# Chunked attention feeding a snake MLP: a V load moved to a later pass, a reordered front, half-tile sines and a split last store

## The chip, the core and the metric

The kernel runs on one core of one Trainium2 chip. The metric is the device time of one execution in microseconds (us). The kernel before took 225.47 us as the median of 8 runs (222.81 to 227.42).

## The reference

Two layers are computed one after the other. The first is attention over chunks of 32 positions: each chunk sees its own 32 keys, 16 to the left, 8 to the right and 8 memory keys. The second is an MLP whose activation is the snake function. B = 4, H = 8, S = 768, D = 64; the MLP has 3072 tokens (4 batches of 768), 512 inputs and 2048 hidden channels.

```
for c in range(nc):                       # chunk 32, left 16, right 8
    k_full = concat([mem_k, k[l_start:r_end]]);  v_full = concat([mem_v, v[l_start:r_end]])
    a = exp(scale * q_c @ k_full.T - max);  a = a / sum(a)
    out[c] = a @ v_full
x = out.transpose(0, 2, 1, 3).reshape(B * S, H * D)
h = x @ w_in
g = h + sin(alpha * h) ** 2 / alpha
y = g @ w_out
```

## The kernel before, in words

The work goes batch by batch. For each batch, the attention makes `xT` (the attention's output, transposed, 128 channels x 4 x 768 tokens); then a pass ("layer", L660) of 16 tiles of 128 hidden channels makes `gT`; then `second` (L545) multiplies `gT` by `w_out` in six tiles of 128 tokens, and each finished 128x512 tile is copied from PSUM to `o_sb` and stored by a DMA from SP's queue. The order of all instructions is written out by hand: a program order per engine, with matmuls of the previous batch's second product fed in small portions (`Feed`, L20) between the steps of the next batch's attention and pass, so that TensorE (PE) always has something to do.

A tile of the pass is: 8 matmuls of 128x384 (`half_first`, L506, four for each half of the tokens) into a pair of PSUM banks; one sine by ScalarE (ACT, L528); one square by ACT (L532), VectorE (DVE, L535) or GpSimd (POOL, L535), chosen by the letters A, V, P of a string; and one DVE operation that forms u*u/alpha + h into `gT` (L538, "the snake" below). PSUM has eight banks; in the first two passes four pairs go around, so tile n + 4 cannot begin before the snake of tile n has read its banks.

**The front (batch 0).** q and k are transposed on PE, scores are taken by unit (head pair, half of the tokens), their exponentials by ACT (L356), products with V on PE (L368), a reciprocal and a multiplication on DVE (L374, L375), a transposition on PE (L385) and a copy into `xT` by ACT (L388). ACT's exponential and sine lie in different tables; L460 loads the sine's between two of the copies. At the end `ahead` (L517) issues the first halves of tiles 0, 1 and 2 on PE; the rest of these tiles follows in the pass.

**Batches 1 to 3.** `attention` (L473) takes scores of eight blocks j of 96 queries (L283), exponentials on ACT (L296), products with V (L309) and the division on DVE. The first five blocks reach `xT` by a transposing DMA from SP, the others by PE and DVE. At its end `ahead` issues the first halves of three tiles. For batches 2 and 3, k and q rows are loaded by 22 DMAs from POOL's queue (`load_rows`, L138) into `kst` and `qst` and turned by 14 transposing DMAs from SP's queue (`cross_steps`, L161, lines 164 and 167) during the pass of the batch before. V is loaded by POOL's DMAs (`load_v`, L177; line 183, and 200 for a tail of batch 3). In the kernel before, the pass of batch 1 starts (L718) by loading the rows of batch 2 and behind them, on the same queue, V of batch 3; the pass of batch 2 loads the rows of batch 3 (L724). `gate` is a one-element copy on POOL that holds these loads back until the attention has written `xT`.

## Time and profile before

| | us |
|---|---|
| median of 8 runs (lowest, highest) | 225.47 (222.81, 227.42) |
| the profiled execution's own time | 225.95 |
| its span, first to last instruction | 224.2 |
| PE / ACT / DVE / POOL busy | 211.2 / 148.0 / 136.0 / 82.5 |
| last matmul of the program | ends about 219.3 |

The execution runs in stages, by the time at which their first matmul starts: the front to 25.7, the pass of batch 0 to 48.2, the attention of batch 1 with the end of batch 0's second product to 74.2, the pass of batch 1 to 97.8, the attention of batch 2 from 99.2 to 115.8, the pass of batch 2 with the second product of batch 1, the attention of batch 3 from 149.2, its pass to 197.4, and the last second product. In rows of the timeline the columns are start, duration, engine, line, operation, tiles, shapes and count, then in brackets the idle time of that engine ahead of the row and what ended it. In windows a row gives the stretch and its length, then busy time (and count) of each engine, the granted TensorE clock, the DMA share and GB/s.

### The profile page before, as it was taken

To read this page: it belongs to the slowest core of one execution; us is meant where nothing else is said; L and a number is where in the kernel's file an instruction comes from. 1 tells how busy PE (TensorE), PEld (TensorE's weight loads), DVE (VectorE), ACT (ScalarE), POOL (GpSimd) and SP (SyncE) were. 2 spreads that over 40 slices of the span, in tenths; PEclk is the share of its full clock that TensorE was granted. 3 is DMA by queue.
4 is the path that set the end of the run, shared out by engine and by line. 5 is a ranking of instruction groups with operands and counts; after the bars stand their busy time and mean duration, and the time that the engine had idled before them with its cause. 6 is when DMAs were issued, how large, how long until landed. Compare 5 with 4: busy or idle time off the path is not lost.

```text
span 224.2 us, 4377 instructions
## 1 busy us (share of the span) xinstructions
PE 211.2 (94%) x1672; PEld 112.7 (50%) x1672; DVE 136.0 (61%) x233; ACT 148.0 (66%) x217; POOL 82.5 (37%) x102
## 2 busy tenths in 40 slices
PE   7999799999999989999599999999999999999991
PEld 2555555545545545544255555544555555544440
DVE  5866559793437689995562875765845764851110
ACT  2558578994778399998546879797928777741101
POOL 8997663795600799800039960000000000000000
PEclk9999999999999999999999999999999999999999
DMA  5999999999999799999969999552410110112121
GB/s 80 166 163 175 207 207 207 200 174 123 101 175 166 68 174 145 159 153 123 171 111 141 130 104 208 132 134 71 115 52 0 47 50 1 47 47 80 64 94 48
DMA packets 98733, 26.96 MB, mean 120 GB/s; under 512 B 86792, under 2 KB 95640, under 8 KB 98712
## 3 DMA queue, kind: packets, MB, share of 16 engines
q0 software_dynamic: 71520, 14.82, 81.2%
q1 hardware_dynamic: 27192, 11.86, 26.8%
q8 instruction: 13, 0.21, 0.4%
q14 instruction: 8, 0.07, 0.1%
HBM read 29.69 MB, written 6.29 MB: 161 GB/s over the span
## 4 chain that ended last, share of the span: by engine, by line
PE 64%; DMA 10%; POOL 7%; SPq 6%; DVE 5%; ACT 4%; issue 2%; DVEq 0%; ACTq 0%; POOLq 0%
PE ps L554 33%; PE ps L508 23%; DMA kT<-kst 5%; DMA q_bf<-in_q_dram 3%; SPq L167 3%; SPq L164 3%; PE ps L283 2%; PE ps L309 2%; DMA kst<-in_k_dram 2%; DVE gT L538 1%; POOL kst L148 1%; ACT u L528 1%; POOL qst L153 1%; POOL kst L143 1%; POOL vw L183 1%
## 5 line engine op out<-in xcount | busy, mean ns | idle before, releaser
L554 PE MATMUL ps<-w_out_sb,gT 128*128 128x512 bf16 x384 | 98.9, 379 | 0.3
L508 PE MATMUL ps<-xT,w_in_sb 128*128 128x384 bf16 x512 | 91.3, 326 | 1.9 <-DVE gT L538 1.3
L538 DVE SCALAR_TENSOR_TENSOR gT<-u,inv_alpha,ps 128x768 bf16<-128x768 f32 x64 | 63.4, 1012 | 24.1 <-ACT u L532 20.0
L528 ACT ACTIVATE u<-ps,alpha_sb 128x768 f32<-128x768 f32 x64 | 56.7, 896 | 26.7 <-PE ps L508 25.8
L508 PEld LDWEIGHTS <-w_in_sb 128*128 128x128 bf16 x512 | 49.6, 98 | 39.7 <-issue 4.2
L554 PEld LDWEIGHTS <-gT 128*128 128x128 bf16 x384 | 34.4, 98 | 31.3 <-issue 0.9
L532 ACT ACTIVATE u<-u 128x768 f32<-128x768 f32 x40 | 33.7, 843 | 1.2
L296 ACT ACTIVATE pt<-ps,biasm 128x256 bf16<-128x256 f32 x72 | 28.7, 473 | 7.2 <-issue 2.8
L567 DVE COPY o_sb<-ps 128x512 f32<-128x512 f32 x17 | 11.7, 690 | 25.3 <-PE ps L554 25.2
L535 DVE TENSOR_TENSOR u<-u 128x768 f32<-128x768 f32 x18 | 17.2, 954 | 6.0 <-ACT u L528 5.9
L183 POOL DMA_DIRECT2D vw<-in_v_dram x15 | 18.1, 1215 | 0.0
L316 DVE TENSOR_TENSOR x_blk<-ps,rinv 96x512 bf16<-96x512 f32 x24 | 16.5, 686 | 1.1 <-DVE rinv L315 0.3
L569 ACT COPY o_sb<-ps 128x512 f32<-128x512 f32 x7 | 4.1, 584 | 19.0 <-PE ps L554 19.0
L336 PE MATMUL ps<-idle 128*128 128x512 bf16 x31 | 10.9, 454 | 1.7 <-DVE vw L596 1.2
L262 ACT COPY kT<-ps 128x672 bf16<-128x672 bf16 x8 | 5.7, 718 | 10.0 <-PE ps L247 7.1
L148 POOL DMA_DIRECT2D kst<-in_k_dram x16 | 11.8, 735 | 0.1
L283 PEld LDWEIGHTS <-kT 64*128 64x128 bf16 x192 | 4.9, 94 | 13.0 <-issue 11.2
L143 POOL DMA_DIRECT2D kst<-in_k_dram x16 | 11.3, 704 | 0.3 <-issue 0.3
L315 DVE RECIPROCAL rinv<-ps 96x8 f32<-96x8 f32 x24 | 4.8, 202 | 10.6 <-PE ps L309 5.4
L309 PEld LDWEIGHTS <-pt 128*128 128x128 bf16 x192 | 9.0, 98 | 4.1
L153 POOL DMA_DIRECT2D qst<-in_q_dram x12 | 10.9, 908 | 0.0
L535 POOL TENSOR_TENSOR u<-u 128x768 f32<-128x768 f32 x6 | 8.9, 1492 | 5.3 <-ACT u L528 5.3
(77 smaller groups left out, 132.8 us busy)
## 6 DMA issues: line engine op xcount, KB each, us to landing
out_dram<-o_sb SPq DMA_DIRECT2D x24, 256.0 KB
w_out_sb<-in_moe_w_out_dram POOLq DMA_DIRECT2D x2, 1024.0 KB, 17.6
w_in_sb<-in_moe_w_in_dram POOLq DMA_DIRECT2D x3, 512.0 KB, 10.1
vw<-in_v_dram POOLq DMA_DIRECT2D x3, 512.0 KB, 10.6
qst<-in_q_dram POOLq DMA_DIRECT2D x12, 128.0 KB, 4.8
vw<-in_v_dram POOLq DMA_DIRECT2D x2, 448.0 KB, 12.4
kst<-in_k_dram POOLq DMA_DIRECT2D x14, 64.0 KB, 5.0
kst<-in_k_dram POOLq DMA_DIRECT2D x14, 56.0 KB, 4.8
```

Of the source, the lines that this page charges most:

```text
L143: nc.gpsimd.dma_start(kst[r0:64, j, :].rearrange("p (h d) -> p h d", d=D), k[b, :, lo + r0:lo + 64, :].rearrange("h p d -> p h d"),)
L148: nc.gpsimd.dma_start(kst[72:72 + n, j, :].rearrange("p (h d) -> p h d", d=D), k[b, :, QW * j + 48:QW * j + 48 + n, :].rearrange("h p d -> ...
L183: nc.gpsimd.dma_start(vw[p0:p1, c0:c1, 0:D], flat[r0:r0 + QW * (c1 - c0)].rearrange("(n t) d -> t n d", t=QW)[0:p1 - p0],)
L296: nc.scalar.activation(pt[:, 0:H * QW].rearrange("p (g e c) -> p g e c", g=2, e=4)[:, :, :, 32 * m:32 * m + 32], sc[:, :, 0:4 * QW].rearra ...
L309: nc.tensor.matmul(otv[:, e, hp, :], pt[:, QW * i:QW * i + P], vws[b % 2][:, 2 * hp + e, j, 0:D + 1],)
L316: nc.vector.tensor_tensor(out=x_blk[:].rearrange("p g e d -> p e g d"), in0=otv[0:QW, :, :, 0:D], in1=rinv[:].unsqueeze(3).to_broadcast([Q ...
L508: nc.tensor.matmul(hT[:, hf, 0:HALF], w_in_sb[:, kt, P * ft:P * ft + P], xT[:, kt, HALF * hf:HALF * hf + HALF], start=(kt == 0), stop=(kt ...
L528: nc.scalar.activation(u[:], hT[:, :, 0:HALF], ACTF.Sin, scale=alpha_sb[:, ft:ft + 1])
L532: nc.scalar.activation(u[:], u[:], ACTF.Square)
L535: eng.tensor_tensor(out=u[:], in0=u[:], in1=u[:], op=ALU.mult)
L538: nc.vector.scalar_tensor_tensor(out=gT[:, ft, :].rearrange("p (e c) -> p e c", e=2), in0=u[:], scalar=inv_alpha[:, ft:ft + 1], in1=hT[:, ...
L554: nc.tensor.matmul(ps[:, bank, :], gT[:, ft, P * s:P * s + P], w_out_sb[:, ft, :], start=(ft == 0), stop=(ft == FT - 1),)
```

## The change

There are four edits.

1. `load_v(3)`, three DMAs of POOL's queue, goes from the pass of batch 1 (behind the rows of batch 2) to the pass of batch 2 (behind its gate, ahead of the rows of batch 3).
2. The last output tile (128 tokens x 512) is made in two halves of 256 columns, each with 16 matmuls, a copy (DVE the first, ACT the second) and a store of its own.
3. `ahead` does more: to the first half of a tile's matmuls it adds, on ACT, the sine and the square of that half; the snakes of these halves stand on DVE at the start of the pass, and `first` then handles only the second half of these tiles. Batches 1 to 3 do so for three tiles, batch 0 for two.
4. In the front, products with V, scores, copies and idle matmuls (`warm`) stand in another order; the sine's table is loaded behind the last ACT copy; the last copy into `xT` goes from ACT to DVE. In the pass of batch 0 the string of squares, the tile at which the ring of PSUM pairs is widened, and the tile at which V of batch 1 is issued (12 instead of 11) change.

```diff
@@ -379,15 +379,13 @@
         )
         return x_blk
 
-    def unit_turn(xT, hp, half, x_blk):
+    def unit_turn(xT, hp, half, x_blk, copy):
         xtp = packed(single(), 4, QW)
         for jj in range(4):
             nc.tensor.transpose(
                 xtp[:, jj, :], x_blk[:, jj].rearrange("p e d -> p (e d)"), ident[0:QW, 0:QW]
             )
-        nc.scalar.copy(
-            xT[:, hp, HALF * half:HALF * half + HALF].rearrange("p (j c) -> p j c", j=4), xtp
-        )
+        copy(xT[:, hp, HALF * half:HALF * half + HALF].rearrange("p (j c) -> p j c", j=4), xtp)
 
     def attention_first(kq, alphas, ahead):
         xT = xp.tile([P, KT, S], BF, name="xT")
@@ -411,8 +409,8 @@
         def pv(*u):
             xb[u] = unit_values(*u, pt[u])
 
-        def x(*u):
-            unit_turn(xT, *u, xb.pop(u))
+        def x(hp, half, copy=nc.scalar.copy):
+            unit_turn(xT, hp, half, xb.pop((hp, half)), copy)
 
         turn_k(0)
         warm(2)
@@ -450,24 +448,26 @@
         warm(1)
         plan(big=(4, 0, 2))
         pv(1, 0)
-        sc(3)
-        units = [(hp, half) for hp in range(1, HP - 1) for half in range(2)]
-        for n in range(1, len(units)):
-            pv(*units[n])
-            warm(1)
-            x(*units[n - 1])
-            if n == 1:
-                nc.scalar.preload_act_table(ACTF.Sin)
-            warm(1)
+        sc_half(3, 0)
+        pv(1, 1)
+        sc_half(3, 1)
+        x(1, 0)
+        pv(2, 0)
         warm(1)
+        x(1, 1)
+        pv(2, 1)
+        warm(2)
+        x(2, 0)
         pv(3, 0)
+        warm(2)
         x(2, 1)
         pv(3, 1)
+        warm(1)
         x(3, 0)
+        nc.scalar.preload_act_table(ACTF.Sin)
         ahead(0, 0, xT)
+        x(3, 1, nc.vector.tensor_copy)
         ahead(1, 0, xT)
-        x(3, 1)
-        ahead(2, 0, xT)
         return xT
 
     def attention(b, stream, shares, lag, crossed, beside=iter(()), beside_from=0):
@@ -514,33 +514,45 @@
 
     begun = {}
 
+    def sine(u, hT, ft, e):
+        nc.scalar.activation(u[:, e], hT[:, e, 0:HALF], ACTF.Sin, scale=alpha_sb[:, ft:ft + 1])
+
     def ahead(ft, hf, xT):
         if ft < 3:
-            begun[ft] = two("big")
-            half_first(begun[ft], ft, hf, xT)
-
-    def first(ft, xT, gT, square, hT=None):
-        if hT is None:
+            hT = two("big")
+            half_first(hT, ft, hf, xT)
+            u = mlp.tile([P, 2, HALF], F32, name="u", bufs=4)
+            e = slice(hf, hf + 1)
+            sine(u, hT, ft, e)
+            nc.scalar.activation(u[:, e], u[:, e], ACTF.Square)
+            begun[ft] = (hT, u)
+
+    def first(ft, xT, square, started=None):
+        e = slice(0, 2)
+        if started is not None:
+            hT, u = started
+            e = slice(1, 2)
+        else:
             hT = two("h")
             half_first(hT, ft, 0, xT)
+            u = mlp.tile([P, 2, HALF], F32, name="u", bufs=4)
         half_first(hT, ft, 1, xT)
-        u = mlp.tile([P, 2, HALF], F32, name="u", bufs=4)
-        nc.scalar.activation(u[:], hT[:, :, 0:HALF], ACTF.Sin, scale=alpha_sb[:, ft:ft + 1])
+        sine(u, hT, ft, e)
 
         def squared():
             if square == "A":
-                nc.scalar.activation(u[:], u[:], ACTF.Square)
+                nc.scalar.activation(u[:, e], u[:, e], ACTF.Square)
             else:
                 eng = nc.vector if square == "V" else nc.gpsimd
-                eng.tensor_tensor(out=u[:], in0=u[:], in1=u[:], op=ALU.mult)
-
-        def finish():
-            nc.vector.scalar_tensor_tensor(
-                out=gT[:, ft, :].rearrange("p (e c) -> p e c", e=2),
-                in0=u[:], scalar=inv_alpha[:, ft:ft + 1], in1=hT[:, :, 0:HALF],
-                op0=ALU.mult, op1=ALU.add,
-            )
-        return squared, finish
+                eng.tensor_tensor(out=u[:, e], in0=u[:, e], in1=u[:, e], op=ALU.mult)
+        return hT, u, e, squared
+
+    def snake(gT, ft, hT, u, e):
+        nc.vector.scalar_tensor_tensor(
+            out=gT[:, ft, :].rearrange("p (e c) -> p e c", e=2)[:, e],
+            in0=u[:, e], scalar=inv_alpha[:, ft:ft + 1], in1=hT[:, e, 0:HALF],
+            op0=ALU.mult, op1=ALU.add,
+        )
 
     def second(i, gT, cut=0):
 
@@ -569,12 +581,32 @@
                 nc.scalar.copy(o_sb[:], ps[:, bank, :])
             nc.sync.dma_start(out[S * i + P * s:S * i + P * s + P, :], o_sb[:])
 
+        def halves(s):
+            for hf in range(2):
+                bank = begin_o()
+                c = slice(256 * hf, 256 * hf + 256)
+                for ft in range(FT):
+                    nc.tensor.matmul(
+                        ps[:, bank, 0:256], gT[:, ft, P * s:P * s + P], w_out_sb[:, ft, c],
+                        start=(ft == 0), stop=(ft == FT - 1),
+                    )
+                    if ft % 2 == 1 and (hf == 0 or ft < FT - 1):
+                        yield
+                kept.remove(bank)
+                o_sb = mlp.tile([P, d_model], F32, name="o_sb", bufs=2)
+                (nc.vector.tensor_copy if hf == 0 else nc.scalar.copy)(o_sb[:, 0:256], ps[:, bank, 0:256])
+                nc.sync.dma_start(out[S * i + P * s:S * i + P * s + P, c], o_sb[:, 0:256])
+
         early = []
         if cut:
             for s in range(2):
                 early.append(begin_o())
                 yield from part(s, early[s], 0, cut)
         for s in range(NSUB):
+            if i == B - 1 and s == NSUB - 1:
+                yield from halves(s)
+                yield
+                break
             bank = early[s] if s < len(early) else begin_o()
             yield from part(s, bank, cut if s < len(early) else 0, FT)
             end_o(s, bank)
@@ -661,35 +693,37 @@
         gT = gTs[i % 2]
         pend = []
         fed = 0
+        for ft in sorted(begun):
+            snake(gT, ft, *begun[ft], slice(0, 1))
         for ft in range(FT):
             begin(ft)
             square = squares[ft % len(squares)]
-            squared, fin = first(ft, xT, gT, square, begun.pop(ft, None))
+            hT, u, e, squared = first(ft, xT, square, begun.pop(ft, None))
             want = to_feed * (ft + 1) // FT
             feed.take(want - fed)
             fed = want
             for due, f in [p for p in pend if p[0] <= ft]:
-                f()
+                snake(gT, *f)
             pend = [p for p in pend if p[0] > ft]
             squared()
-            pend.append((ft + (2 if square == "P" else 1), fin))
+            pend.append((ft + (2 if square == "P" else 1), (ft, hT, u, e)))
         for due, f in pend:
-            f()
+            snake(gT, *f)
         feed.add(second(i, gT, 0 if i else 13), NSUB * FT)
 
     prs = []
 
     def begin_0(ft):
-        if ft == 3:
-            plan(h=[6] + rings["big"])
-        if ft == 11:
+        if ft == 2:
+            plan(h=[rings["big"][0], 6] + rings["big"][1:])
+        if ft == 12:
             load_v(1)
             send_memv(1)
             send_memv(2)
         if ft == 15:
             prs.extend(pair_up(kq1[n // HP], n % HP) for n in range(4))
 
-    layer(0, xT, "VPPAPAVPPAPAVAAA", begin_0, 0)
+    layer(0, xT, "VPPAPAVPAVPPAAAA", begin_0, 0)
     last4 = rings["h"]
     plan(one=(last4[0], last4[0] + 1), t=(last4[1], last4[1] + 1), big=last4[1:])
     put_memk(1)
@@ -718,12 +752,12 @@
             if i == 1 and ft == 0:
                 nc.gpsimd.tensor_copy(gate[:], xT[0:1, 0, QW * 6 - 1:QW * 6])
                 load_rows(2)
-                load_v(3)
                 for _ in crossings:
                     pass
             if i == 2:
                 if ft == 0:
                     nc.gpsimd.tensor_copy(gate[:], xT[0:1, 0, QW * 6 - 1:QW * 6])
+                    load_v(3)
                     load_rows(3)
                 if ft >= 1:
                     next(crossings, None)
```

On POOL, this is the piece between the rows of batch 2 and those of batch 3 (`gate` is the one-element copy, `vw_88` the buffer of V for odd batches, `kst` the rows of k; in the kernel before the lines are 183, 200 and 726):

```order
 L143 DMA kst<-in_k_dram 64x8x64
 L148 DMA kst<-in_k_dram 48x8x64
+L759 COPY gate<-xT 1x1
 L183 DMA vw_88<-in_v_dram 64x64x64
 L183 DMA vw_88<-in_v_dram 56x63x64
 L200 DMA vw_88<-in_v_dram 48x64
-L726 COPY gate<-xT 1x1
 L143 DMA kst<-in_k_dram 48x8x64
 L148 DMA kst<-in_k_dram 56x8x64
```

The three V loads now stand behind the gate of batch 2's pass and ahead of the first rows of batch 3.

On ACT, from the last exponentials of the front to the first tiles of the pass, first as before (388 is the copy into `xT`, 460 the table load, 528 the sine, 532 the square):

```order
L356 ACTIVATE pt_first<-ps 128x768 x2
L388 COPY xT<-ps 128x384
L460 ACT_TABLE_LOAD
L388 COPY xT<-ps 128x384 x5
L528 ACTIVATE u<-ps,alpha_sb 128x768 x4
L532 ACTIVATE u<-u 128x768
```

and in the changed kernel (467 is the table load, 518 the sine, 527 the square inside `ahead`):

```order
L356 ACTIVATE pt_first<-ps 128x768 x2
L388 COPY xT<-ps 128x384 x5
L467 ACT_TABLE_LOAD
L518 ACTIVATE u<-ps,alpha_sb 128x384
L527 ACTIVATE u<-u 128x384
L518 ACTIVATE u<-ps,alpha_sb 128x384
L527 ACTIVATE u<-u 128x384
L518 ACTIVATE u<-ps,alpha_sb 128x384 x2
L518 ACTIVATE u<-ps,alpha_sb 128x768 x2
```

The table load stands behind five copies, not between the first and the others, and the first sines and squares are of 384 columns.

On DVE, from the last copy into `xT` of batch 1 into its pass, before (535 is the square, 538 the snake):

```order
L329 COPY xT<-ps 128x4x96
L535 TENSOR_TENSOR u<-u 128x768
L538 SCALAR_TENSOR_TENSOR gT<-u,inv_alpha,ps 128x768 x2
L535 TENSOR_TENSOR u<-u 128x768
L538 SCALAR_TENSOR_TENSOR gT<-u,inv_alpha,ps 128x768 x2
```

and in the changed kernel (547 the square, 551 the snake):

```order
L329 COPY xT<-ps 128x4x96
L551 SCALAR_TENSOR_TENSOR gT<-u,inv_alpha,ps 128x384 x3
L547 TENSOR_TENSOR u<-u 128x384
L551 SCALAR_TENSOR_TENSOR gT<-u,inv_alpha,ps 128x384 x2
L547 TENSOR_TENSOR u<-u 128x384
L551 SCALAR_TENSOR_TENSOR gT<-u,inv_alpha,ps 128x384
L551 SCALAR_TENSOR_TENSOR gT<-u,inv_alpha,ps 128x768
L547 TENSOR_TENSOR u<-u 128x768
```

Three half snakes stand ahead of the first square; nothing on DVE waits for a whole tile until they are through.

## The prediction

> **What bounds the kernel now.** I read the windows first, to see where TensorE (PE) is not busy, then PE's timeline for the waits inside those windows, then the chain of waits and the DMA view.
>
> ```profile
> 20.00:32.00 12.00, 10.34 (x113) 6.33 (x112) 6.56 (x13) 8.36 (x13) 7.38 (x9) 1.00 1.30 204
> ...
> 78.00:98.00 20.00, 18.98 (x114) 10.86 (x112) 18.24 (x20) 19.07 (x24) 16.70 (x21) 1.00 1.97 157
> 99.00:112.00 13.00, 10.52 (x127) 4.99 (x125) 8.19 (x15) 10.17 (x23) 0.00 (x0) 1.00 1.74 148
> 113.00:149.00 36.00, 36.00 (x228) 19.85 (x223) 22.70 (x30) 27.32 (x34) 16.71 (x23) 1.00 1.27 135
> ...
> 219.00:224.00 5.00, 0.19 (x1) 0.00 (x0) 0.00 (x0) 0.59 (x1) 0.00 (x0) 0.95 0.14 54
> ```
>
> The second number is the length, the third PE's busy time. From 113 us on PE is gapless: nothing that the change does there can gain, it can only cost. What can be had lies in four places: the front (1.66 us idle of 12), the pass of batch 1 (1.02 of 20, with DVE and ACT almost full as well), the attention of batch 2 (2.48 of 13), and the 4.9 us behind the last matmul. Each of the four edits aims at one of them.
>
> **Edit 1: V of batch 3 leaves the pass of batch 1.** PE's rows of scores, for batch 2 (first, second, seventh, eighth block) and for batch 3 (first, last):
>
> ```profile
> 99.16 0.34 PE L283 MATMUL ps<-qT,kT 64*128 64x96 bf16 x8
> 100.68 0.34 PE L283 MATMUL ps<-qT,kT 64*128 64x96 bf16 x8 [0.21 <-DVE gT L538]
> ...
> 109.62 0.35 PE L283 MATMUL ps<-qT,kT 64*128 64x96 bf16 x8 [1.23 <-DVE o_sb L567]
> ...
> 112.25 0.34 PE L283 MATMUL ps<-qT,kT 64*128 64x96 bf16 x8 [1.28 <-DMA kT<-kst]
> ...
> 149.19 0.34 PE L283 MATMUL ps<-qT,kT 64*128 64x96 bf16 x8
> ...
> 159.35 0.34 PE L283 MATMUL ps<-qT,kT 64*128 64x96 bf16 x8
> ```
>
> First to last block takes 13.09 us for batch 2 and 10.16 for batch 3, with the same matmuls between. Of the 2.93 us, 0.21 are a wait for a snake; 2.7 are two waits for turned rows of k and q (the copy named in the first is done long before; the transposition of the sixth q tile is what is late there too). Why are they late?
>
> ```profile
> 100.49 1.29 SPq L167
> ...
> 101.90 10.30 DMA kT<-kst
> ...
> vw<-in_v_dram POOLq DMA_DIRECT2D x2, 448.0 KB, 12.4
> ...
> vw<-in_v_dram POOLq DMA_DIRECT2D x1, 441.0 KB, 21.0
> ...
> 90.79 3.36 POOL L183 DMA_DIRECT2D vw<-in_v_dram  x2
> 94.13 0.56 POOL L200 DMA_DIRECT2D vw<-in_v_dram  x1
> ...
> 70.43 2.51 SPq L492 DMA_TRANSPOSE xT<-x_blk  x2
> ...
> 74.19 0.81 PE L508 MATMUL ps<-xT,w_in_sb 128*128 128x384 bf16 x4 [0.18 <-DMA xT<-x_blk]
> ```
>
> The last transposition is issued at 101.90 and lands 10.30 us later, while V of batch 3 (issued 90.8 to 94.7, 21 us to landing for its second part) fills the same DMA engines. With those engines nearly free, the second of the two transpositions issued from 70.43 on (about 71.7) lets PE go at 74.19: 2.5 us. So without V the last one lands near 104.4. It is needed at 99.16 + 10.16 = 109.3, or 108.1 if the pass ahead gets 1.25 us shorter (below): a cover of 3.7 us. I take the whole **2.7 us**. Ends: 2.9 (the 0.21 too), 0 (the rows of batch 2, not V, hold the transpositions up).
>
> Its new place, in batch 2's pass:
>
> ```profile
> 115.55 0.18 POOL L726 COPY gate<-xT 1x1 bf16<-1x1 bf16 x1 [20.85 <-DVE xT L329]
> ...
> 132.03 0.64 POOL L148 DMA_DIRECT2D kst<-in_k_dram  x1
> ...
> kst<-in_k_dram POOLq DMA_DIRECT2D x14, 56.0 KB, 4.8
> ...
> 148.35 1.21 SPq L164 DMA_TRANSPOSE kT<-kst  x1
> ...
> POOL w_in_sb L220 <- DMA q_bf<-in_q_dram: 0.9, 1, 0.9
> ```
>
> Three V issues put the rows back by 3.36 + 0.56 = 3.9 us at POOL. More comes from completion semaphores: the program has eight for POOL's DMAs, so each issue waits for the landing of the one eight before it (the last row is such a wait). The sixth row DMA then waits for V's first part: 12.4 us by the median of V alone. The 22 row DMAs took 17.1 us behind the gate (to 132.67), 0.78 each; now the sixth is issued 12.4 us behind the gate, the seventh with V's second part at 14.1, fifteen more at 0.78: the last at 25.8, landing 4.8 later, at 30.6 (146.2 on the old clock). SP turns them in order and issued the last at 148.35, that is after this moment; landing 2.5 us later, 8.5 us ahead of its need at 159.35. V itself is first used after the scores of 149.19 and is there by about 130. Behind the transpositions on SP stand stores of batch 1's output, with two `o_sb` buffers: they leave when they left before. So I cost the new place at **0**; what hides it is that 8.5 us, and beyond it each us is one us of PE.
>
> **Edits 3 and 4 in the front.** Tile 4 of batch 0's pass waits for the snake of tile 0:
>
> ```profile
> 21.85 1.28 ACT L460 ACT_TABLE_LOAD   x1
> 23.15 0.86 ACT L388 COPY xT<-ps 128x384 bf16<-128x384 bf16 x2
> ...
> 21.89 0.20 DVE L374 RECIPROCAL rinv<-ps 96x8 f32<-96x8 f32 x1
> ...
> 25.63 0.69 DVE L375 TENSOR_TENSOR x_blk<-ps,rinv 96x512 bf16<-96x512 f32 x1
> ...
> 27.63 0.48 ACT L388 COPY xT<-ps 128x384 bf16<-128x384 bf16 x1 [1.23 <-PE ps L385]
> 28.94 3.50 ACT L528 ACTIVATE u<-ps,alpha_sb 128x768 f32<-128x768 f32 x4 [0.82 <-PE ps L508]
> ...
> 30.94 1.01 DVE L538 SCALAR_TENSOR_TENSOR gT<-u,inv_alpha,ps 128x768 bf16<-128x768 f32 x1
> ...
> 32.01 16.07 PE L508 MATMUL ps<-xT,w_in_sb 128*128 128x384 bf16 x96 [0.51 <-DVE gT L538]
> ...
> 48.23 4.48 PE L554 MATMUL ps<-w_out_sb,gT 128*128 128x512 bf16 x20
> ```
>
> Before: last division ends 26.32, last copy 28.1, first sine 28.94, snake 31.95. After, step by step: a unit costs DVE about 0.93 (0.20, a short gap, 0.69); with V products ahead of scores and no table load between copies, I place the last division's end at 25.3. PE turns it (0.15), DVE copies (0.35): xT is whole at 26.1 and the second halves start at 26.2, not 28.1. ACT copies until 25.2 and loads its table until 26.5; two half sines and half squares at 0.5 take it to 28.5; the second half's sine ends at 29.0, square 29.65, snake 30.25. Tile 4 starts at 30.3: **1.7 us** earlier. The same 12 tiles follow (16.2 us to 48.23), so the pass ends that much earlier. Half operations go by these rows:
>
> ```profile
> L388 ACT COPY xT<-ps 128x384 bf16<-128x384 bf16 x8 | 3.7, 480 | 2.7 <-PE ps L385 2.7
> L329 DVE COPY xT<-ps 128x384 bf16<-128x384 bf16 x9 | 3.2, 352 | 1.8 <-PE ps L326 1.8
> ```
>
> Ends: 1.9 (the 1.66 us that PE idles there and a warm-up matmul), 0.3 (the new order saves only a warm-up matmul).
>
> A page speaks against this: the Trainium skill (ScalarE: Activation LUTs, "What ACT_TABLE_LOAD costs") gives a table switch 1283 ns plus a drain of about 1380. The load above took 1.28 us and the next copy began 0.02 us behind it, so this trace shows no drain; by the page the front's term would be 0.3.
>
> **Edit 3 in the passes.** Pass of batch 1:
>
> ```profile
> 77.94 0.90 ACT L528 ACTIVATE u<-ps,alpha_sb 128x768 f32<-128x768 f32 x1 [3.85 <-PE ps L508]
> 78.87 0.96 DVE L535 TENSOR_TENSOR u<-u 128x768 f32<-128x768 f32 x1 [1.83 <-ACT u L528]
> 81.00 2.76 PE L508 MATMUL ps<-xT,w_in_sb 128*128 128x384 bf16 x16 [0.50 <-DVE gT L538]
> ```
>
> ACT idles 3.85 us and DVE 1.83 just before a stretch in which both are the bound. The change moves into these idle times three half sines and three half squares (ACT) and three half snakes (DVE). From 78 on ACT then has, per tile of the three, about 0.9 - 0.5 less sine, and half a square less for one: 3 x 0.4 = 1.2, and about 0.4, less some 0.35 of start costs that halves pay twice: **1.25 us**. DVE is rid of more (three half snakes and two half squares, 2.5 us), so ACT limits. Ends: 0.4 (start costs eat it), 2.2 (DVE's share counts). In the passes of batches 2 and 3 the halves cost ACT about 0.1 us a tile; it is busy 27.32 of 36 us there, which hides it: 0.
>
> **Edit 2, the tail.**
>
> ```profile
> 219.27 0.59 ACT L569 COPY o_sb<-ps 128x512 f32<-128x512 f32 x1 [6.32 <-PE ps L554]
> ...
> SPq L773 <- DMA out_dram<-o_sb: 2.5, 1, 2.5
> ```
>
> Twice as many matmuls of half the columns are the same PE time. The last copy halves, 0.59 to about 0.35; the 2.5 us wait for the last store loses something between 0 and half. Against it: the second half's buffer is the one of the tile before, whose store ends about when it is wanted (up to 0.25 late). I take **0.35**, ends -0.1 and 1.4. The Trainium skill (DMA: Bandwidth & Descriptors, the fixed and variable costs) gives about 2 us fixed plus bytes / 436e9 per second; 128 KB less would be 0.3 us, and the term 0.55.
>
> **Sum.** 2.7 + 1.7 + 1.25 + 0.35 = 6.0 us: span 224.2 to 218.2. The profiled execution's own time is 225.95, 0.5 above the median of the runs, 225.47; on the median's scale the forecast is **219.5 us**.
>
> **Rivals.**
> (a) *V in front of the rows makes batch 3 late.* If V takes there what it took before, 22.7 us (issue at 90.79, the second part at about 92.5 and 21.0 to its landing), the rows 17.1 + 4.8 behind it, and the last transposition 10.3, it lands 54.9 us behind the gate; needed at 43.8 (115.55 to 159.35). PE loses 11.1 us, net +5.1: 230.6 us. It costs once the last k lands later than 43.8, and makes the kernel slower from 49.8 on. For it: DMA is busy through most of this window. Against: its 10.3 needs V and transpositions at once, and V goes first. 4%.
> (b) *The wait in batch 2 stays*, because rows and transpositions hold each other up without V and the pass ahead ends sooner: gain 3.3, 222.2 us. For it: SP needs about 1.4 us per transposition and issues the last at 101.9 anyway. 10%.
> (c) *ACT bounds the front*: table load, half sines and squares in a row push the first snake to where it was. Front 0.3, sum 4.6: 220.9 us. A drain behind the table load, as the page has it, would do exactly this. 17%.
> (d) *The halves do nothing in batch 1's pass* (start costs): sum 5.2, 220.3 us. 8%.
>
> **How the numbers follow.** Forecast 61%. It, (c) and (d) are faster by over 1% (2.3 us, about what a measurement of this kernel can tell from no change); so is most of (b). That gives 0.89 faster, 0.07 the same (part of (b), and several low ends at once), 0.04 slower. The forecast's own ends together make a gain of about 3 to 8; with the scatter of the medians the range is 217.3 to 222.6, and it holds (b) to (d).
>
> **What the new profile would show.** Right: the scores of batch 2's last two blocks without a wait, 10.2 to 10.4 us from first to last; the transpositions landing within 4 us; tile 4 of batch 0 at about 30.3; ACT's first sine of batch 1's pass before PE's second halves, and that pass about 1.2 us shorter; PE gapless in batches 2 and 3 as before; about 4.5 us behind the last matmul. Wrong: a DMA wait at the scores of batch 3, DVE waiting on `o_sb` for a store behind a transposition, a gap on ACT behind the table load, or the score waits of batch 2 still there with V gone.

## The result, and the profile after

The changed kernel took 220.0 us as the median of 11 runs (218.24 to 221.48), beside 225.09 us for the kernel before in the same sessions (32 runs, 222.81 to 227.57). The ratio is 0.9782 with a 95% interval of 0.9751 to 0.9813: 4.9 us faster, between 4.2 and 5.6. Ratios leave out the runs that are over 1.5% above the fastest of their kernel, and medians are over all its runs, so the two can differ, most for the first experiment, where two of six runs are left out. The profiled executions, 225.95 before (span 224.2) and 219.54 after (span 217.8), lie 6.4 us apart, 1.3 more than the medians: the one of before is 0.9 above its median and the one of after 0.5 below.

The same windows as in the prediction, for the changed kernel and moved with its stages (stretch, length, busy PE, PEld, DVE, ACT, POOL, clock, DMA share, GB/s):

```profile
20.00:32.00 12.00, 11.77 (x118) 7.41 (x117) 7.81 (x17) 10.32 (x18) 7.33 (x9) 1.00 1.29 205
76.00:95.00 19.00, 18.93 (x116) 11.07 (x114) 17.40 (x22) 18.34 (x25) 12.85 (x18) 1.00 2.03 157
96.00:109.00 13.00, 12.79 (x161) 6.54 (x162) 9.31 (x19) 12.13 (x27) 0.00 (x0) 1.00 0.76 115
110.00:146.00 36.00, 36.00 (x219) 19.49 (x218) 23.54 (x29) 29.41 (x42) 20.40 (x25) 1.00 2.02 144
```

PE's idle time fell from 1.66 to 0.23 us in the front, to 0.07 in this part of batch 1's pass, and from 2.48 to 0.21 in the attention of batch 2. Three of the four places are closed. PE's rows name the stage ends: tile 4 of batch 0 (inside the x44), the second product of batch 0, the start of batch 1's pass, first and last scores of batch 2, first scores of batch 3, and the first matmuls of batch 3's pass.

```profile
25.21 7.32 PE L508 MATMUL ps<-xT,w_in_sb 128*128 128x384 bf16 x44
32.68 13.72 PE L508 MATMUL ps<-xT,w_in_sb 128*128 128x384 bf16 x80 [0.15 <-DVE gT L551]
46.23 4.05 PE L566 MATMUL ps<-w_out_sb,gT 128*128 128x512 bf16 x18
...
72.34 0.81 PE L508 MATMUL ps<-xT,w_in_sb 128*128 128x384 bf16 x4 [0.32 <-DMA xT<-x_blk]
...
95.93 0.34 PE L283 MATMUL ps<-qT,kT 64*128 64x96 bf16 x8
...
106.36 0.34 PE L283 MATMUL ps<-qT,kT 64*128 64x96 bf16 x8
...
143.26 0.34 PE L283 MATMUL ps<-qT,kT 64*128 64x96 bf16 x8
...
158.15 0.81 PE L508 MATMUL ps<-xT,w_in_sb 128*128 128x384 bf16 x4 [1.01 <-DMA xT<-x_blk]
```

The scores of batch 2 now take 106.36 - 95.93 = 10.43 us from first to last block, 2.66 less than before. Batch 1's pass starts 1.85 us earlier (74.19 before), and the attention behind it 3.23 us (99.16 before), so that pass is 1.38 us shorter. The last row is new: PE waits for `xT` ahead of batch 3's pass, a wait that the profile before does not have. There the same matmuls were:

```profile
162.91 0.81 PE L508 MATMUL ps<-xT,w_in_sb 128*128 128x384 bf16 x4
```

From the first scores of batch 3 to these matmuls it was 162.91 - 149.19 = 13.72 us; now it is 158.15 - 143.26 = 14.89. So 1.17 us are lost there.

How that wait comes about stands in SP's queue, first of before, then of after:

```profile
124.26 0.69 SPq L157 DMA_DIRECT2D kst<-memk_st  x1
129.17 1.21 SPq L164 DMA_TRANSPOSE kT<-kst  x1
...
154.85 5.15 SPq L492 DMA_TRANSPOSE xT<-x_blk  x4
```

```profile
119.11 0.69 SPq L157 DMA_DIRECT2D kst<-memk_st  x1
127.76 1.38 SPq L164 DMA_TRANSPOSE kT<-kst  x1
...
147.78 1.21 SPq L164 DMA_TRANSPOSE kT<-kst  x1
...
150.25 5.11 SPq L492 DMA_TRANSPOSE xT<-x_blk  x4
```

One small DMA, the memory keys into `kst` (L157, 64 KB), stands behind eight DMAs of memory values and is what SP's first row transposition waits for. From its issue to that transposition 4.9 us pass before and 8.65 after, beside V of batch 3: the DMA share is 1.88 from 124 to 129 us before and 3.12 from 119 to 128 after. From there SP works through 14 transpositions and the stores between them with hardly a gap, about 1.2 to 1.4 us of SP's time for each transposition, and the transpositions of `xT` (L492) stand behind them in the same queue. Counted from the first scores of batch 3, the last row transposition is issued 0.84 us ahead of them before (148.35 against 149.19) and 4.52 us behind them after (147.78 against 143.26); the first `xT` transposition slips from 5.66 to 6.99 us behind them, 1.33 us; PE's wait is the part of it that the slack of before does not cover. POOL's rows are late too, as reckoned; one of two waits for V's landing, with its idle time in brackets:

```profile
124.90 0.69 POOL L143 DMA_DIRECT2D kst<-in_k_dram  x1 [4.98 <-DMA vw<-in_v_dram]
```

The front, the start of batch 1's pass and the tail, in the timeline of ACT and DVE, and then in SP's waits (total us, times, longest):

```profile
24.85 1.28 ACT L467 ACT_TABLE_LOAD   x1
26.14 0.58 ACT L518 ACTIVATE u<-ps,alpha_sb 128x384 f32<-128x384 f32 x1
...
27.31 0.61 DVE L551 SCALAR_TENSOR_TENSOR gT<-u,inv_alpha,ps 128x384 bf16<-128x384 f32 x1 [1.47 <-ACT u L527]
...
29.52 1.28 DVE L551 SCALAR_TENSOR_TENSOR gT<-u,inv_alpha,ps 128x384 bf16<-128x384 f32 x2
...
73.19 0.58 ACT L518 ACTIVATE u<-ps,alpha_sb 128x384 f32<-128x384 f32 x1 [1.09 <-PE ps L508]
...
214.50 0.37 ACT L597 COPY o_sb<-ps 128x256 f32<-128x256 f32 x1 [6.32 <-PE ps L589]
```

```profile
SPq L807 <- DMA out_dram<-o_sb: 1.1, 1, 1.1
```

The sine starts 0.01 us behind the table load. The snake of tile 0's first half is the row at 27.31; that of its second half is the first of the two at 29.52 and ends at about 30.2. Tile 4 did not wait for it: 28 of the 44 matmuls from 25.21 on stand ahead of tile 4, one every 0.1625 us, so its first half starts at 29.76 and its second at 30.41. The wait for the last store, 2.5 us before, is 1.1. From the last copy's start to the end of the span 217.8 - 214.50 = 3.3 us pass, where before 224.2 - 219.27 = 4.9 did: 1.6 us. How much of this is the change's, the second experiment asks.

### The profile page after: what moved, and what is told of

Read it like the earlier page. It is cut to its first block, busy times and chain, and to the rows that moved or that the text cites. A ratio compares the mean times of both kernels' runs of the same rounds, so it can differ in the third digit from the quotient of the medians.

```text
span 217.8 us, 4457 instructions
## 1 busy us (share of the span) xinstructions
PE 209.9 (96%) x1687; PEld 114.2 (52%) x1687; DVE 137.7 (63%) x246; ACT 153.1 (70%) x238; POOL 82.4 (38%) x102
## 4 chain that ended last, share of the span: by engine, by line
PE 69%; POOL 9%; DMA 8%; DVE 6%; ACT 3%; issue 3%; DVEq 0%; ACTq 0%; POOLq 0%
PE ps L566 35%; PE ps L508 27%; DMA w_in_sb<-in_moe_w_in_dram 5%; POOL vw L183 3%; PE ps L283 3%; DMA xT<-x_blk 3%; DVE gT L551 3%; ACT u L518 2%; PE ps L309 2%; POOL u L547 2%; PE ps L589 2%; DVE u L547 1%; POOL w_in_sb L220 1%; POOL q_bf L172 1%; POOL k_bf L172 1%
## 5 line engine op out<-in xcount | busy, mean ns | idle before, releaser
L566 PE MATMUL ps<-w_out_sb,gT 128*128 128x512 bf16 x368 | 95.5, 380 | 0.2
L551 DVE SCALAR_TENSOR_TENSOR gT<-u,inv_alpha,ps 128x768 bf16<-128x768 f32 (+1 forms) x75 | 65.8, 895 | 23.0 <-ACT u L544 16.1
L518 ACT ACTIVATE u<-ps,alpha_sb 128x768 f32<-128x768 f32 (+1 forms) x75 | 59.4, 801 | 20.9 <-PE ps L508 20.3
L566 PEld LDWEIGHTS <-gT 128*128 128x128 bf16 x368 | 32.8, 98 | 29.1 <-issue 0.5
L544 ACT ACTIVATE u<-u 128x768 f32<-128x768 f32 (+1 forms) x40 | 31.5, 787 | 1.2
L547 DVE TENSOR_TENSOR u<-u 128x768 f32<-128x768 f32 (+1 forms) x18 | 16.0, 887 | 1.7 <-ACT u L518 1.6
L316 DVE TENSOR_TENSOR x_blk<-ps,rinv 96x512 bf16<-96x512 f32 x24 | 16.5, 686 | 0.8
L143 POOL DMA_DIRECT2D kst<-in_k_dram x16 | 11.1, 694 | 5.0 <-DMA vw<-in_v_dram 5.0
L581 ACT COPY o_sb<-ps 128x512 f32<-128x512 f32 x6 | 3.5, 584 | 12.7 <-PE ps L566 12.7
L336 PE MATMUL ps<-idle 128*128 128x512 bf16 x30 | 10.0, 441 | 1.3 <-DVE vw L628 1.2
L547 POOL TENSOR_TENSOR u<-u 128x768 f32<-128x768 f32 (+1 forms) x6 | 8.7, 1464 | 5.8 <-ACT u L518 5.8
```

The source lines that it names most:

```text
L316: nc.vector.tensor_tensor(out=x_blk[:].rearrange("p g e d -> p e g d"), in0=otv[0:QW, :, :, 0:D], in1=rinv[:].unsqueeze(3).to_broadcast([Q ...
L518: nc.scalar.activation(u[:, e], hT[:, e, 0:HALF], ACTF.Sin, scale=alpha_sb[:, ft:ft + 1])
L544: nc.scalar.activation(u[:, e], u[:, e], ACTF.Square)
L547: eng.tensor_tensor(out=u[:, e], in0=u[:, e], in1=u[:, e], op=ALU.mult)
L551: nc.vector.scalar_tensor_tensor(out=gT[:, ft, :].rearrange("p (e c) -> p e c", e=2)[:, e], in0=u[:, e], scalar=inv_alpha[:, ft:ft + 1], i ...
L566: nc.tensor.matmul(ps[:, bank, :], gT[:, ft, P * s:P * s + P], w_out_sb[:, ft, :], start=(ft == 0), stop=(ft == FT - 1),)
```

## The experiments

The theory after the traces: four gains (2.66 in the attention of batch 2, 1.85 in the front, 1.38 in batch 1's pass, something at the tail) less a cost of 1.17 at V's new place, through SP's queue. The rivals: the new place is free and the wait there only shows that PE came earlier; the store at the end was late by chance in the profile of before; the stages of one edit hide behind those of another. The last column of the table is the difference of an experiment's ratio from 0.9782, times 225 us.

| kernel | median, us | ratio to before, 95% interval | against the changed kernel, us |
|---|---|---|---|
| V of batch 3 back | 223.96 | 0.9893 (0.9842 to 0.9945) | +2.5 |
| last tile whole | 220.54 | 0.9797 (0.9771 to 0.9822) | +0.3 |
| whole tiles in batches 1 to 3 | 220.95 | 0.9815 (0.9778 to 0.9852) | +0.7 |
| batch 0 as before | 222.3 | 0.9869 (0.9844 to 0.9894) | +2.0 |
| V of batch 3 left out | 219.13 | 0.977 (0.9721 to 0.9819) | -0.3 |
| memory keys first | 219.25 | 0.9771 (0.9722 to 0.9819) | -0.2 |
| V in batch 2's attention | 227.32 | 1.0137 (1.0089 to 1.0185) | +8.0 |
| V back, with idle matmuls | 223.09 | 0.9912 (0.9872 to 0.9952) | +2.9 |
| V behind the rows of batch 3 | 219.35 | 0.9752 (0.9701 to 0.9802) | -0.7 |
| V's move alone, on the kernel before | 224.14 | 0.9957 (0.9928 to 0.9985) | |
| new front, whole tiles in batch 0 | 220.42 | 0.9798 (0.9757 to 0.9839) | +0.4 |
| memory keys first and V behind the rows | 222.2 | 0.988 (0.9828 to 0.9932) | +2.2 |

The intervals are 0.5 to 1.2 us to either side, and the changed kernel's own is 0.7, so differences below about 1 us are read from the traces and not from the medians.

### V of batch 3 back in batch 1's pass

```diff
                 load_rows(2)
+                load_v(3)
...
-                    load_v(3)
                     load_rows(3)
```

> The changed kernel with V of batch 3 back behind the rows of batch 2, everything else kept. Theory (the move gains 2.7 us in the attention of batch 2 and costs 1.2 us at the first matmuls of batch 3's pass, where PE waits for transpositions of xT): 1.5 us slower than the changed kernel, about 221.5 us; the scores of batch 2 take 13.1 us from first to last block again, and the 1.0 us wait for xT ahead of batch 3's pass is gone. Rival (the move is free at its new place, as predicted, and the 1.0 us wait comes from PE being earlier): 2.7 us slower, about 222.7 us, and a wait for xT of about 1 us stays.

2.5 us slower by the ratio and 4.0 between the medians, above the theory's 1.5 either way. The wait for `xT` ahead of batch 3's pass is gone, as the theory had it, but the price at batch 2's scores has grown. PE's row, and windows of 2 us behind it:

```profile
108.73 0.50 PE L283 MATMUL ps<-qT,kT 64*128 64x96 bf16 x8 [2.48 <-DMA qT<-qst]
```

```profile
108.00:110.00 2.00, 1.27 (x17) 0.88 (x18) 0.00 (x0) 0.68 (x2) 0.00 (x0) 0.50 1.49 224
...
116.00:118.00 2.00, 2.00 (x18) 1.14 (x14) 1.46 (x4) 0.79 (x2) 1.67 (x4) 1.00 0.04 3
```

Before, the wait came in two pieces of 1.23 and 1.28 us, with PE at work between them. Here it is one of 2.48, and behind it the granted clock is 0.50 for some 6 us: a block of scores takes 0.50 us instead of 0.34. Half the work of 6 us is about 3 us. From the first scores of batch 2 to the first matmul of its pass this execution takes 19.58 us (96.75 to 116.33), the changed kernel 14.00 (95.93 to 109.93), so the price there is 5.6 us and not 2.7. Five of the six runs, this one among them, had a mean clock of 0.985 to 0.992 and took 222.0 to 224.8 us; the one at 1.0 took 220.94. So this run cannot tell theory from rival by its time alone.

### The last output tile whole

```diff
-            if i == B - 1 and s == NSUB - 1:
-                yield from halves(s)
-                yield
-                break
```

> The changed kernel with the last output tile whole again. Theory (the halves are worth what the two profiled executions differ by behind the last matmul, 1.6 us): 221.6 us, and 4.9 us from the last copy's start to the end. Rival (the halves are worth 0.35 to 0.7 us as predicted, and the store at the end of the profiled execution of before was late by chance): about 220.5 us, and about 3.7 to 4.0 us from the last copy's start to the end.

```profile
214.81 0.59 ACT L581 COPY o_sb<-ps 128x512 f32<-128x512 f32 x1 [6.32 <-PE ps L566]
```

0.3 us by the ratio, with about 0.9 to either side. The span is 218.7, so 3.9 us pass behind that copy's start: 0.6 more than with halves, but 1.0 less than in the profile of before with the very same last tile. A third execution with the whole tile, that of V's move alone (below), ends like the one of before, SP's wait for the last store included:

```profile
SPq L773 <- DMA out_dram<-o_sb: 2.3, 1, 2.3
```

Its last copy starts at 216.62 and its span is 221.3: 4.7 us. The eleven profiled executions with halves all take 3.2 to 3.3. So the halves are worth 0.6, 1.4 or 1.6 us in the traces and 0.3 by the ratio. The theory's 221.6 us did not come, but the rival's claim that before's last store was late by chance is not shown either: two of three executions with the whole tile end that late, and what makes the third shorter stays open.

### Whole tiles in batches 1 to 3

```diff
-                ahead(1, 0, xT)
+                ahead(1, 0, xT, False)
...
-                ahead(0, 0, xT)
+                ahead(0, 0, xT, False)
...
-        ahead(2, 0, xT)
+        ahead(2, 0, xT, False)
```

With `False`, `ahead` issues the matmuls alone, and sine, square and snake of that tile are whole in the pass.

> The changed kernel with the sines, squares and snakes of the three tiles ahead whole again in batches 1 to 3; batch 0 keeps its halves. Theory (the halves relieve ACT in the pass of batch 1 by 1.25 to 1.4 us and nothing elsewhere): about 221.4 us, the pass of batch 1 takes 23.5 us from its first matmul to that of the second product, as before, and PE stays gapless in the pass of batch 2. Rival (start costs eat it, and the shorter pass came from the changed order of the other batches): 220.0 to 220.4 us and 22.2 us for the pass.

```profile
72.84 0.81 PE L508 MATMUL ps<-xT,w_in_sb 128*128 128x384 bf16 x4 [0.46 <-DMA xT<-x_blk]
...
79.65 2.76 PE L508 MATMUL ps<-xT,w_in_sb 128*128 128x384 bf16 x16 [0.50 <-DVE gT L557]
...
97.80 0.34 PE L283 MATMUL ps<-qT,kT 64*128 64x96 bf16 x8
```

From the first matmul of batch 1's pass to the first scores of batch 2 it is 97.80 - 72.84 = 24.96 us, and 95.93 - 72.34 = 23.59 with halves: 1.37 us. The wait of 0.50 for a snake is back at the place where the prediction quoted it. By the ratio the time moved by 0.7 us, with an interval of 0.8 to either side, which does not contradict 1.37. PE is gapless in batch 2's pass with and without halves.

### Batch 0 as before

```diff
-        ahead(0, 0, xT)
-        x(3, 1, nc.vector.tensor_copy)
-        ahead(1, 0, xT)
+        ahead(1, 0, xT, False)
+        x(3, 1)
+        ahead(2, 0, xT, False)
...
-    layer(0, xT, "VPPAPAVPAVPPAAAA", begin_0, 0)
+    layer(0, xT, "VPPAPAVPPAPAVAAA", begin_0, 0)
```

> The changed kernel with batch 0 as before: old order of the front, table load between two copies, no halves of sines there, three tiles ahead, old squares and old tile for V of batch 1. Theory (the front is worth 1.85 to 2.0 us): about 221.9 us, and the second product of batch 0 begins at 48.2 instead of 46.4. Rival (part of it is given back later, since the pass of batch 0 waits for loads of w_out or V of batch 1 anyway): less than 1 us slower, 220.0 to 221.0 us.

```profile
48.61 3.61 PE L572 MATMUL ps<-w_out_sb,gT 128*128 128x512 bf16 x16 [0.55 <-DVE gT L557]
```

2.0 us slower, and the second product of batch 0 starts at 48.61 instead of 46.23. The gain of the front is kept to the end: the rival, that loads of `w_out` or V of batch 1 would take part of it back, falls.

### V of batch 3 left out

```diff
-                    load_v(3)
                     load_rows(3)
```

> The changed kernel without any load of V of batch 3 (batch 3 then multiplies with the V of batch 1 and its own memory values, so its output is another). Theory (V ahead of the rows makes SP's row transpositions late, and these hold up the xT transpositions of batch 3, which stand behind them in SP's queue): the wait of PE for xT ahead of batch 3's pass is gone, 1.2 us faster than the changed kernel, about 218.9 us; SP's first row transposition starts at 121 or before instead of 127.8. Rival (SP's 14 row transpositions of about 1.35 us and the memory rows are late by themselves, V or not): the wait stays at 0.8 us or more, 219.8 us or above.

```profile
118.31 0.69 SPq L157 DMA_DIRECT2D kst<-memk_st  x1
123.50 1.22 SPq L164 DMA_TRANSPOSE kT<-kst  x1
...
142.14 1.21 SPq L164 DMA_TRANSPOSE kT<-kst  x1
```

The wait at batch 3's pass is gone. SP's first row transposition starts at 123.5, 4.3 us earlier than in the changed kernel, though not at 121: it still follows the memory keys, by 5.2 us. The last one is issued 5.6 us earlier. So V holds up the start of SP's row transpositions, and through it everything that stands behind them on SP. The median is 0.9 us lower; the ratio moved by 0.3 only, within its interval.

### The memory keys first

```diff
             if i == 1:
+                rows_memk(3)
                 send_memv(3)
```

`rows_memk` is the DMA of L157, taken out of `load_rows(3)`.

> The changed kernel with one DMA moved on SP's queue: the memory keys of batch 3 (kst from memk_st) go ahead of the eight DMAs of its memory values instead of behind them. Theory (this DMA, issued at 119.1 behind the eight and landing at 127 while V holds the DMA engines, is what SP's first row transposition waits for): that one starts at 122 to 124 instead of 127.8, the wait for xT ahead of batch 3's pass shrinks from 1.0 us to below 0.3, about 219.0 us. Rival (the rows from POOL, whose last is issued at 135, are the limit): SP ends its row transpositions at 147 as before, no gain, 219.9 to 220.1 us.

```profile
126.09 1.21 SPq L168 DMA_TRANSPOSE kT<-kst  x1
...
145.61 1.21 SPq L168 DMA_TRANSPOSE kT<-kst  x1
```

The wait for `xT` ahead of batch 3's pass is gone here too, with V in its new place and only SP's order changed. The step between was not as expected: the first row transposition starts at 126.1 and not at 122 to 124, since it now waits 4.0 us for rows of k that V holds up at POOL. So both are late beside V, the memory keys by 1.7 us more than the rows (127.76 against 126.09). The last row transposition is issued 2.2 us earlier (145.61 against 147.78), and that is enough all the same. The median is 0.75 us lower than the changed kernel's; the ratio moved by 0.2.

### V in the attention of batch 2

```diff
             feed.take(6)
+            if i == 1:
+                nc.gpsimd.tensor_copy(gate[:], kTs[0][0:1, 0, P * 7:P * 7 + 1])
+                load_v(3)
...
-                    load_v(3)
                     load_rows(3)
```

> The changed kernel with V of batch 3 at a third place: in the attention of batch 2, behind a one-element copy on POOL that reads the last turned k tile of batch 2, so neither beside the row transpositions of batch 2 nor ahead of the rows of batch 3 at their gate. Theory (only what V stands beside matters): both waits are gone, the scores of batch 2 within 10.5 us and no wait for xT ahead of batch 3's pass, 1.2 us faster than the changed kernel, about 218.9 us. Rival (V then collides with the five xT transpositions of batch 2, and PE waits at the first matmuls of its pass): 0.5 to 2 us slower than the changed kernel.

The theory fails, and the rival holds with four times its upper price: 8.0 us slower. V is issued by POOL from 103.12 on, beside the five `xT` transpositions of batch 2 (SP, from 102.63). PE's row:

```profile
117.00 1.44 PE L508 MATMUL ps<-xT,w_in_sb 128*128 128x384 bf16 x4 [6.15 <-DMA xT<-x_blk]
```

In the changed kernel the same transpositions are issued at 101.87 and PE takes up the pass at 109.93 without a wait. Beside V, PE waits 6.15 us for them, and the granted clock is 0.50 in the windows from 114 to 120. The stretch from 96 to 109 us has the lowest DMA share of the four windows of the changed kernel above (0.76), but the few transfers in it are waited for.

### V back, with five idle matmuls in the long wait

```diff
         sc = two(kind)
+        if b == 2 and j == 6:
+            for _ in range(5):
+                nc.tensor.matmul(sc[:, 0, :], idle[:, 0:P], idle[:])
```

> V of batch 3 back behind the rows of batch 2 as in the first run, and five idle matmuls of 512 columns on PE ahead of the seventh block of scores of batch 2, where PE waited 2.5 us in one piece and the granted clock then stood at 0.5 for 6 us. Theory (the drop of the clock follows the long wait): the wait is cut to about 1.4 us by the 1.1 us of idle matmuls, the clock stays at 1.0 from 106 to 116, and the median falls to 220.9 to 221.5 us with a small scatter. Rival (the drop has another cause, or the first run's slower half was chance): the clock drops here too and the median stays at 222.6 to 224.

```profile
104.79 0.35 PE L286 MATMUL ps<-qT,kT 64*128 64x96 bf16 x8 [0.94 <-DMA qT<-qst]
...
105.97 1.24 PE L283 MATMUL ps<-idle 128*128 128x512 bf16 x5
...
108.70 0.35 PE L286 MATMUL ps<-qT,kT 64*128 64x96 bf16 x8 [1.48 <-DMA qT<-qst]
...
110.25 0.34 PE L286 MATMUL ps<-qT,kT 64*128 64x96 bf16 x8 [0.21 <-DMA kT<-kst]
...
114.89 0.81 PE L511 MATMUL ps<-xT,w_in_sb 128*128 128x384 bf16 x4 [0.92 <-DMA xT<-x_blk]
```

The first half of the theory holds: the clock stays at 1.00 in every window from 102 to 118, and 11 of 12 runs had a mean clock of 0.998 to 1.0. The second half does not: the median is 223.09, above the expected 220.9 to 221.5. The rows show where it went. The waits for turned rows and for `xT` add up to 0.94 + 1.48 + 0.21 + 0.92 = 3.55 us, and with the 1.24 of idle matmuls, which fill a wait, to 4.8. Before it was 2.66 (13.09 against the 10.43 of the changed kernel) with the same loads in the same order. What differs is when PE comes: its first scores follow SP's first row transposition by 16.5 us before (82.66 to 99.16) and by 14.5 here (81.37 to 95.90). With V in its old place, time won in batch 1's pass is handed back at batch 2's scores.

### V behind the rows of batch 3

```diff
-                    load_v(3)
                     load_rows(3)
+                    load_v(3)
```

> The changed kernel with V of batch 3 behind the rows of batch 3 instead of ahead of them, in the same pass. Theory (a transposition that is issued while V fills the DMA engines lands 8 to 11 us late, and V needs some 21 us): V is issued at about 131 to 135 and lands at about 155, the row transpositions of 128 to 143 run beside it, PE waits at the last scores of batch 3 or at its first products with V, 3 to 8 us in all: 223 to 228 us. Rival (the rows are through early enough, and SP's queue is earlier by the 8 us that V held it up): no wait at scores or values, 219 us.

```profile
123.58 1.22 SPq L164 DMA_TRANSPOSE kT<-kst  x1
```

```profile
vw<-in_v_dram POOLq DMA_DIRECT2D x1, 441.0 KB, 18.7
```

The theory fails and the rival holds: no wait of PE for a DMA from batch 3's scores on, and 219.35 us. V, issued at 127.07 to 131, was through in 18.7 us, at about 147.5, just when its first product starts. The row transpositions, begun at 123.6 and issued until 145.4, were still in time. How little room there is shows the last run.

### V's move alone, on the kernel before

```diff
                 load_rows(2)
-                load_v(3)
...
+                    load_v(3)
                     load_rows(3)
```

> The kernel before with the move of V of batch 3 alone, without the three other edits. Theory (the move is worth the 2.7 us of waits at batch 2's scores less the 1.2 us wait for xT ahead of batch 3's pass, whatever the other edits do): 1.5 us faster than before, ratio 0.993, and a wait of about 1 us for xT there. Rival (the gain of the move depends on the other edits: with the pass of batch 1 as long as before, the need comes later and the waits that the move removes are smaller than in the changed kernel, where putting V back cost 2.5 to 3 us): nothing is different, also 0.993, but the three other edits without it gain 2.4 us (first run) where their stages sum to 3.6, so that the two cannot be added; the sum of this gain and that one is then about 1 us short of the whole 5.0.

```profile
98.98 0.34 PE L283 MATMUL ps<-qT,kT 64*128 64x96 bf16 x8
...
109.42 0.34 PE L283 MATMUL ps<-qT,kT 64*128 64x96 bf16 x8
...
160.27 0.81 PE L508 MATMUL ps<-xT,w_in_sb 128*128 128x384 bf16 x4
```

1.0 us faster than before (0.3 to 1.6). The scores take 10.44 us, the same 2.65 less, and in this execution there is no wait at batch 3's pass at all. The profiled execution, 223.08, was the fastest of twelve; what the others lose, some 1 us more, no trace here shows. The parts do not seem to add: by the ratios, edits 2 to 4 without the move gain 2.4 (first experiment), the move alone 1.0, all four 4.9. The missing 1.5 us is about as large as the intervals together, so this sum alone does not prove it; the first experiment and the one with idle matmuls show a mechanism, waits that grow when PE comes earlier.

### The new front with whole tiles in batch 0

```diff
-        ahead(0, 0, xT)
+        ahead(0, 0, xT, False)
         x(3, 1, nc.vector.tensor_copy)
-        ahead(1, 0, xT)
+        ahead(1, 0, xT, False)
```

> The changed kernel with whole tiles in batch 0: the new order of the front stays (table load behind the last ACT copy, last copy on DVE), but the sines, squares and snakes of tiles 0 and 1 are not halved; batches 1 to 3 keep their halves. Theory (in the front the order carries the gain, and the halves little): 220.0 to 220.5 us, and the second product of batch 0 begins within 0.4 us of the changed kernel's 46.2 to 46.4. Rival (half sines and squares right behind the table load carry it, since ACT is the limit there): 1 us or more slower, 221 us, with PE waiting 1 us for the snake of tile 0.

```profile
32.27 1.01 DVE L557 SCALAR_TENSOR_TENSOR gT<-u,inv_alpha,ps 128x768 bf16<-128x768 f32 x1 [2.10 <-POOL u L553]
...
33.33 14.82 PE L508 MATMUL ps<-xT,w_in_sb 128*128 128x384 bf16 x88 [1.65 <-DVE gT L557]
47.99 2.32 PE L572 MATMUL ps<-w_out_sb,gT 128*128 128x512 bf16 x10
```

The two measures disagree. In the trace PE waits 1.65 us for a snake and the second product starts at 47.99, as the rival has it (0.45 us of that was lost earlier: its table load is at 25.29 and not at 24.85). The cause is not the rival's, though. The wait is tile 5's for the snake of tile 1 (40 matmuls are through ahead of it), and that snake waited for its square on POOL, not for ACT. Tile 1's sine ended at about 28.8; POOL was held until 30.16 by the issue of a load of memory keys, which itself waited 1.95 us for a load of `w_in`, and began the square at 30.75. With halves, half of that square is done on ACT. The median is only 0.4 us above the changed kernel's, as the theory has it; the profiled execution, 221.45, was the slowest of six. Which part of the front's 1.9 us the halves carry stays open; that order and halves together carry it, the fourth experiment shows.

### Memory keys first and V behind the rows

> The changed kernel with two edits that each took 0.7 to 0.9 us: the memory keys of batch 3 ahead of its memory values on SP's queue, and V of batch 3 behind the rows of batch 3 on POOL's. Theory (both remove the same wait, that of PE for xT ahead of batch 3's pass, so they do not add): 219.0 to 219.5 us, ratio to before 0.973 to 0.977; SP's first row transposition starts at about 121, and no wait ahead of batch 3's pass. Rival (the wait was larger in the runs that have no profile, and the two together leave more slack than each): 218.5 us or less.

Its edits are those of the two experiments above, together. Both sides miss: 222.2 us, slower than either edit alone.

```profile
120.09 1.22 SPq L168 DMA_TRANSPOSE kT<-kst  x1
```

```profile
149.94 0.40 PE L313 MATMUL ps<-vw,pt 128*128 128x65 bf16 x8 [2.30 <-DMA vw<-in_v_dram]
```

SP's row transpositions start at 120.1, 3.5 us earlier than with V behind the rows alone. V's second part needs 20.9 us to land instead of 18.7, and PE waits 2.30 us for it at batch 3's first product. Why V is later stays open: V is issued at almost the same time (127.31 and 127.07), and from then on fewer row transpositions are issued here (9) than there (11). Three of the six runs had a mean clock of 0.992 besides. There is no wait for `xT`, as expected; PE waits for V instead.

No version here beats the changed kernel by more than the intervals. The memory keys first (219.25) and V behind the rows (219.35) have the lower medians, and neither shows the wait that the changed kernel has.

## Why the prediction was right, and where it was not

**Edit 1, the waits at batch 2's scores: 2.7, measured 2.66.** The transposition rows and the DMA landings behind it were read rightly, and V was the cause: with V back the waits return (first and eighth kernel of the table), and with V's move alone they go. Rival (b) falls. What the prediction did not see is that the term hangs on the others: 2.7 is what the waits cost before, and 4.8 is what they cost once PE comes earlier, or 5.6 with the drop of the clock.

**Edit 1, the new place: 0, measured 1.17 in the profiled execution.** This is the term that failed. The step was the sentence that the last transposition lands "8.5 us ahead of its need at 159.35". Two things are wrong in it. It reckoned when POOL's rows are there and found this before the 148.35 at which SP issued its last transposition before, and took 148.35 as unchanged. But SP's start hangs on the memory keys, 64 KB that now land beside V: 8.65 us to the first transposition instead of 4.9. SP then has no slack to catch up. And it named the wrong consumer: the cover was counted to batch 3's last scores, but behind the rows on SP stand the `xT` transpositions of batch 3, which are late as soon as SP is. What is queued behind was followed on POOL and, on SP, as far as the stores; L492 was left out. The sign "PE gapless in batches 2 and 3 as before" failed with it. POOL's own delay was sized well, though from a misread row: the 448 KB with 12.4 us are second parts of V for two batches, while the first part has 512 KB and landed in 8.6 us after the change; the sixth row DMA was issued 9.4 us behind the gate and not 12.4, the seventh 15.2 and not 14.1, the last 26.5 and not 25.8. In kind this is rival (a), V ahead of the rows making batch 3 late, at a tenth of its price of 11.1 us and at another wait. The wait varies: 1.01 us in the changed kernel, 0.28 with the last tile whole, 0.90 with whole tiles in batches 1 to 3, 0.77 with batch 0 as before, 0.75 with the new front and whole tiles, none with V's move alone. Without V, or with V behind the rows, or with the memory keys first, it is gone, so V's place ahead of the rows and SP's queue are its cause; why it is absent with V's move alone stays open.

**The front: 1.7, measured 1.85 to 2.0.** The last division ends at 24.75 (25.3 predicted), and the snake of tile 0 at about 30.2 (30.25). But the last step was not as described, and here the size is right in part by luck: tile 4 did not have to wait for that snake. Its first half starts at 29.76, when only the snake of tile 0's first half (27.31 to 27.92) is through, its second half at 30.41. So tile 4 came 2.25 us earlier than before (32.01), and some of this was given back at tile 6, where PE waits 0.15 us for the snake of tile 2. Rival (c) falls: no gap behind the table load, neither in the trace of before nor here. The drain that the Trainium skill gives (ScalarE: Activation LUTs, "What ACT_TABLE_LOAD costs") would have stood between 26.13 and 26.14; this trace has none there.

**Edit 3 in batch 1's pass: 1.25, measured 1.38.** ACT's first sine is at 73.19, ahead of PE's second halves at 75.23, as described; rival (d) falls by the third experiment's trace.

**The tail: 0.35, measured 0.3 by the ratio (0.9 to either side) and 0.6, 1.4 or 1.6 by the traces.** So the term was right or too small, and the runs do not settle which. The sign, "about 4.5 us behind the last matmul", was too long: it is 3.3.

**The sum.** 2.66 + 1.85 + 1.38 - 1.17 = 4.72 us, and with 0.3 to 1.6 for the tail 5.0 to 6.3, beside 4.9 by the ratio, 5.1 between the medians and 6.4 between the profiles. The forecast gain of 6.0 was too large by about the one term that was taken as 0. That the changed kernel's median, 220.0, lies only 0.5 from the forecast 219.5 is in part luck: the kernel before came out at 225.09 here and not at the 225.47 from which the forecast was counted.

## What to carry to other kernels

When a load moves on one queue, follow every queue that has to wait for something it slows, down to the small DMA at its head, and ask what stands behind that in order; the first late consumer need not be the one that the load serves. Gains that bring an engine earlier to the same transfer can be handed back there until that transfer is earlier too, so the value of such edits need not be the sum of their values alone. And before the end of a profile is used as a price, look how two or three other executions end.

## What the runs showed of the hardware

A single wait of PE of about 2.5 us was followed by a lower granted clock: 0.50 for some 6 us behind 2.48 us of wait, in the run with V back, while waits of 1.2 to 1.5 us with work between left it at 1.00. One of 2.30 us left it at 1.00 too, in the profiled execution of the last experiment. The Trainium skill (TensorE: Matmul & The Clock Gate, "What's actually happening") puts the idle window at about 3.4 us, free-running; here less idle time than one such window was enough, and with 1.24 us of idle matmuls in the wait the clock stayed up. Such a wait can have a second price that its row does not show: by an estimate, 6 us at half speed are about 3 us of lost work, more than the 2.48 of the wait.

Transposing DMAs and a large load on another queue were late beside each other. `xT` of batch 2, issued from 101.87 on, was there without V when PE came at about 110; with V issued beside it, PE waited 6.15 us for it. V's second part in turn landed in 12.5 us in the changed kernel, where SP's row transpositions started behind it (127.76 against 124.9):

```profile
vw<-in_v_dram POOLq DMA_DIRECT2D x1, 441.0 KB, 12.5
```

Where they ran beside it, it took 21.0 us (before), 18.7 (V behind the rows) and 20.9 (with the memory keys first as well). Other loads ran beside V too, so these numbers do not give the transpositions' share.
